# Two fused feed-forward layers behind linear attention on one core: phase 0's out products two units behind, x parts as jobs, phase 1 in another block order, x tiles moved in SBUF

## The chip, the cores and the metric

The kernel runs on one core of one Trainium2 chip. The metric is the device time of one execution in microseconds (us), lower is better: the median of the runs. TensorE is called PE here, VectorE DVE, ScalarE ACT, GpSimd POOL, and SyncE, which here issues DMAs, SP.

## The reference

All inputs are float32. Attention has 8 batches, 8 heads, 576 positions and 64 columns a head, and no softmax; then come two gated feed-forward layers on 4608 tokens of 512 columns, with 1536 hidden columns.

```python
kv = einsum('bhsd,bhse->bhde', k, v)
out = einsum('bhsd,bhde->bhse', q, kv)
x = out / sqrt(mean(out*out, -1) + 1e-6) * g_norm      # then 4608 x 512
x = (sigmoid(x @ moe_w_gate) * (x @ moe_w_val)) @ moe_w_out
y = (silu(x @ moe2_w_gate) * (x @ moe2_w_val)) @ moe2_w_out
```

## The kernel before, in words

**Tiling.** The 4608 tokens are 9 blocks of 512. There are four phases over all blocks (`PH`): phase 0 does hidden columns 0 to 767 of the first layer, phase 1 columns 768 to 1535 of it, phases 2 and 3 the same for the second layer. Each operand is split into a rounded part and a remainder (hi and lo), and each product is three matmuls, lo·hi, hi·lo and hi·hi (`PASSES`). Phase 0 multiplies plainly (`gv_plain`, `part_plain`); phases 1 to 3 do gate and value with seven 2x2 products in place of eight (`gv_win`), and phases 2 and 3 the out product too.

**A unit of phase 0** is one block and one slice of 128 hidden columns, six units a block. Its 24 matmuls (L920) fill two PSUM banks of a ring of four, gate and value; attention's small products take banks of the same ring. ACT makes the sigmoid of the gate bank (L928, tile sg), DVE multiplies it with the value bank (L930), and `split` (L394) then makes the unit's h: hi by ACT (L395), lo by DVE (L373). Only after both ops have read them are the unit's two banks free. The out product of a unit, 12 matmuls (L1104, tile o, from h and wo), is written behind the next unit's gate and value matmuls: `tail` holds the one unit that is still without its out product. There is room for three units' h.

**Order on the engines.** Each engine runs its instructions in order. In blocks 4 to 8 of phase 0 the code sets the order on ACT, DVE and POOL, and a scheduler that of PE and SP; from phase 1 on the code sets PE's order too. The code's own order has two sources. The weights of phases 1 to 3 are rounded and combined by 780 jobs (load, ACT, DVE, POOL, store), which `pump` gives out one at a time: an account (`clock`, `free`, `ready`) keeps estimated times of the engines, and a job is given to an engine once its inputs are expected and it wouldn't wait there. Some jobs may go to DVE or to POOL. The other source are queues of steps with due times; they ask no account. One of them, `xq`, makes x.

**x in phase 0.** Attention writes x of a block to DRAM (`xd`). `seven_steps` loads it in four quarters (tile xl, issued on ACT's own DMA queue, L865), splits each into hi (ACT) and lo (DVE), and for phase 1 subtracts quarters from each other (tile xl, DVE) and stores four results in `x7` (tile name xs, L880). Blocks 3 to 8 do this when they are prepared for phase 0; blocks 0 to 2 are loaded a second time for it, behind blocks 4, 5 and 6.

**x in phases 1 to 3.** Three tiles x0, x1 and x2 hold seven combinations, hi and lo: x0 those named 11, 21 and 22, x1 T1 and T2, x2 T3 and T4. Each of the seven products of a unit reads one combination with 12 matmuls (L1001), x streaming as the moving operand and a weight tile wgv loaded as the stationary one. In the built program x0 begins at byte 163,776 of each partition and x1 at 176,064, both multiples of 64; x2 begins at 221,152, 32 bytes past a multiple of 64. All wgv tiles of these phases begin on multiples of 64.

Of the kernel before, what the change touches and what calls it, by code (L numbers as in the profile page):

```python
# [20 lines left out]
def attention_two_ffn(ctx: ExitStack, tc: tile.TileContext, q, k, v, g_norm, weights, out):  # L21
# [247 lines left out]
    def tok_c(tau):  # L269
        if tau >= XT:  # L270
# [4 lines left out]
            j, c = divmod(tau, TPB)  # L275
            for i in range(P // SQ):
# [11 lines left out]
        j, c = divmod(tau, TPB)  # L288
        cs = slice(c * P, (c + 1) * P)
# [61 lines left out]
    WOUT = (2, 3)  # L351
    phase_of = {(f, m0 + i): (ph, i) for ph, (f, m0, n, _) in enumerate(PH) for i in range(n)}
# [145 lines left out]
    class Job:  # L498
        def __init__(self, does, f, *keys, new=None):
            self.does, self.f, self.keys, self.new = does, f, set(keys), new  # L500
# [24 lines left out]

    def sides():
        if "L" in late:
            return ("B", "C") if now[0] < tick_of(*ASIDE_TO) else ()
# [47 lines left out]
    def pump():  # L576
# [170 lines left out]
    def begin_small():  # L747
# [3 lines left out]
        for z in jobs:  # L751
            if z.group.side is None and z.group not in fresh:
# [53 lines left out]
    def x_load(ph, j, b):  # L806
        k, i = x_at(b)
        h, l = [x_tiles(ph, j)[k][:, i + e] for e in range(2)]
        if PH[ph][0]:
# [39 lines left out]
    def x_steps(ph, j):  # L849
        if PH[ph][3]:  # L850
            return [z for b in (0, 4, 3, 5, 1, 2, 6) for z in (lambda b=b: x_load(ph, j, b), nop)]
        th = seven_steps(j, True, j > 2)
        return th + [nop] + seven_steps(j - 4, False, True) if j in (4, 5, 6) else th

    def seven_steps(j, use_, keep):
        st = {}
        if keep:
            x7[j] = dr.tile([P, 4 * DM], F32, name=f"xs{j}")

        def L(i, n):  # L860
            def run():
                for t in range((j + 1) * TPB):
                    att.need(t)
                st[i, n] = wk.tile([P, 2, HB], F32, tag="xl", bufs=3, name="xl")
                nc.scalar.dma_start(out=st[i, n], in_=xd[0, j][:, 2 * i:2 * i + 2, n * HB:(n + 1) * HB])  # L865
                moved(0.25)
            return run

        def S(i, n):
            def run():  # L870
                hi, lo = [t[:, 2 * i:2 * i + 2, n * HB:(n + 1) * HB] for t in x_tiles(0, j)]
                split(hi, lo, st[i, n])
            return run if use_ else nop

        def D(o, a, b):
            return lambda: sub(st[o], st[a], st[b])

        def store(i, n, o):
            def run():
                nc.sync.dma_start(out=x7[j][:, (o - 3) * DM:(o - 2) * DM], in_=st[i, n].rearrange("p k a -> p (k a)"))  # L880
                moved(0.25)
            return run

        if not keep:
            return [L(0, 0), L(0, 1), L(1, 1)] + [nop] * 6 + [S(0, 0), L(1, 0), nop, S(0, 1), nop, S(1, 1), nop, nop, S(1, 0)]
        return [nop] * LEAD + [L(0, 0), L(0, 1), L(1, 1)] + [nop] * 4 + [S(0, 0), S(0, 1), D((0, 0), (0, 1), (0, 0)), S(1, 1), store(0, 0, 3), D((0, 1), (1, 1), (0, 1)), nop, store(0, 1, 5), L(1, 0),
                D((0, 0), (1, 1), (0, 0)), nop, store(0, 0, 4), nop, S(1, 0), D((1, 0), (1, 0), (0, 0)), nop, store(1, 0, 6)]

# [22 lines left out]
    def gv_plain(ph, j, m, tick):  # L911
# [22 lines left out]
        split(t[:, 0], t[:, 1], sg)  # L934
# [748 lines left out]
```

## Time and profile before

| | us |
|---|---|
| time, median of 3 runs (1797.91 to 1800.07) | 1798.28 |
| time of the profiled execution | 1802.5 |
| its span, first to last instruction | 1800.7 |
| PE busy in it | 1768.0 |
| DVE, ACT and POOL busy | 1221.9, 707.4, 886.4 |

The span is nearly all PE work, so what counts is where PE doesn't run or runs slowly. A matmul's busy time in the rows is its whole passage through the engine, which overlaps with the next one's; the pace is the distance between starts.

### The profile page before, as it was taken

The numbers are of one execution on the slowest core, as the hardware profiler recorded it, in microseconds if no ns is written. First come the engines' busy times: TensorE is split into PE (matmuls) and PEld (weight loads), VectorE is DVE, ScalarE is ACT, GpSimd is POOL, SyncE is SP. The second block draws the span as 40 slices with busy tenths as digits, with TensorE's granted clock in tenths as the row PEclk, the third lists the DMA queues.
The fourth block names the chain that finished last, engine by engine and source line by source line (L and its number), as shares of the span: only waits on it lengthen the run. The fifth ranks groups of instructions, "written<-read, shape, count | busy, mean of one in ns | idle before, by whom it ended". The sixth has DMA issues, their size and how long they took to land.

```text
span 1800.7 us, 33917 instructions
## 1 busy us (share of the span) xinstructions
PE 1768.0 (98%) x12844; PEld 1646.1 (91%) x12844; DVE 1221.9 (68%) x1947; ACT 707.4 (39%) x1535; POOL 886.4 (49%) x960
## 2 busy tenths in 40 slices
PE   7899999999999999999999999999999999999998
PEld 6788888877789999999999999999999999999998
DVE  6764666675674788887775766666665666666665
ACT  4653333233333434443433433333333433333332
POOL 1653455653541467677663444444443444444444
PEclk9999999999999999999999999999999999999999
DMA  9958887669758565656559522222229523223322
GB/s 282 279 162 231 193 236 221 176 198 311 258 189 301 187 216 192 230 180 216 202 205 348 191 65 66 65 66 66 65 90 327 169 89 89 89 89 89 88 89 71
DMA packets 288164, 309.51 MB, mean 172 GB/s; under 512 B 96384, under 2 KB 213504, under 8 KB 287744
## 3 DMA queue, kind: packets, MB, share of 16 engines
q1 hardware_dynamic: 265984, 291.08, 51.0%
q10 hardware_dynamic: 22016, 16.26, 3.1%
q8 instruction: 101, 1.65, 0.4%
q14 instruction: 63, 0.52, 0.1%
HBM read 194.28 MB, written 112.98 MB: 171 GB/s over the span
## 4 chain that ended last, share of the span: by engine, by line
PE 85%; DMA 5%; DVE 4%; POOL 2%; issue 2%; ACT 2%; SPq 1%; ACTq 0%; DVEq 0%; POOLq 0%
PE gv L1001 44%; PE o L1141 14%; PE gv L920 11%; PE o L1119 8%; PE o L1104 6%; PE ops L230 1%; DMA x<-xc 1%; DMA raw<-in_moe_w_out_dram 1%; PE kvps L178 1%; DMA xl<-xd 1%; DMA qm<-in_q_dram 0%; DVE xl L373 0%; DMA aside<-in_moe_w_gate_dram 0%; DMA aside<-in_moe_w_val_dram 0%; POOL aside L651 0%
## 5 line engine op out<-in xcount | busy, mean ns | idle before, releaser
L1001 PE MATMUL gv<-x,wgv 128*128 128x256 f32 x6804 | 827.9, 282 | 3.3 <-ACT u L1010 1.6
L1001 PEld LDWEIGHTS gv<-x,wgv 128*128 128x128 f32 x6804 | 820.4, 191 | 6.3 <-ACT u L1010 1.8
L920 PE MATMUL gv<-x,wgv 128*128 128x512 f32 x1296 | 316.1, 395 | 5.7 <-ACT x L292 2.7
L920 PEld LDWEIGHTS gv<-x,wgv 128*128 128x128 f32 x1296 | 240.9, 189 | 57.7 <-DVE sg L930 4.2
L823 DVE TENSOR_TENSOR x<-x 128x512 fp32r<-128x512 f32 x155 | 147.2, 970 | 45.2 <-ACT x L819 41.3
L1104 PE MATMUL o<-h,wo 128*128 128x512 f32 x648 | 166.5, 401 | 5.9 <-ACT h L395 5.2
L377 DVE TENSOR_TENSOR u<-u,gv 128x512 f32<-128x512 f32 x162 | 110.9, 684 | 85.1 <-ACT h L1044 46.6
L1104 PEld LDWEIGHTS o<-h,wo 128*128 128x128 f32 x648 | 121.3, 191 | 34.7 <-ACT h L395 6.4
L970 ACT ACTIVATE w<-v 128x256 f32<-128x256 f32 x81 | 33.9, 418 | 248.3 <-DVE v L377 244.8
L819 ACT ACTIVATE x<-x 128x512 fp32r<-128x512 f32 x189 | 113.6, 620 | 29.7 <-DMA x<-xc 11.7
L1119 PE MATMUL o<-h,wob 128*128 128x512 f32 x432 | 102.1, 392 | 0.0
L1045 POOL TENSOR_TENSOR spare<-w,spare 128x256 fp32r<-128x256 f32 x54 | 40.8, 755 | 114.2 <-ACT spare L1044 114.2
L1045 POOL TENSOR_TENSOR he<-w,he 128x256 fp32r<-128x256 f32 x54 | 41.0, 759 | 113.7 <-ACT he L1044 113.7
L1045 POOL TENSOR_TENSOR he<-g,he 128x256 fp32r<-128x256 f32 x54 | 50.7, 958 | 92.2 <-ACT he L1044 82.4
L1119 PEld LDWEIGHTS o<-h,wob 128*128 128x128 f32 x432 | 79.8, 188 | 16.6
L1045 POOL TENSOR_TENSOR spare<-g,spare 128x256 fp32r<-128x256 f32 x54 | 50.4, 953 | 90.4 <-ACT spare L1044 90.4
L1010 ACT ACTIVATE u<-gv 128x512 f32<-128x512 f32 x81 | 48.3, 597 | 110.5 <-PE gv L1001 107.5
L1141 PE MATMUL o<-arena,h 128*128 128x256 f32 x636 | 82.9, 279 | 0.0
L377 DVE TENSOR_TENSOR v<-g,gv 128x512 f32<-128x512 f32 x81 | 55.6, 687 | 39.5 <-PE gv L1001 34.8
L970 ACT ACTIVATE v<-g 128x256 f32<-128x256 f32 x81 | 33.9, 418 | 120.9 <-DVE g L377 120.9
L395 ACT ACTIVATE h<-sg 128x512 fp32r<-128x512 f32 x54 | 34.0, 630 | 116.3 <-DVE sg L930 111.5
L1141 PEld LDWEIGHTS o<-arena,h 128*128 128x128 f32 x636 | 78.0, 188 | 0.0
(194 smaller groups left out, 2910.5 us busy)
## 6 DMA issues: line engine op xcount, KB each, us to landing
wgv<-wd SPq DMA_DIRECT2D x72, 448.0 KB, 7.5
x<-xc SPq DMA_DIRECT2D x126, 256.0 KB, 2.8
pl<-pd SPq DMA_DIRECT2D x80, 256.0 KB, 4.2
xc<-pl SPq DMA_DIRECT2D x63, 256.0 KB, 2.3
raw<-in_moe_w_out_dram SPq DMA_DIRECT2D x22, 512.0 KB, 5.0
wd<-stage SPq DMA_DIRECT2D x44, 256.0 KB, 2.2
xl<-xd ACTq DMA_DIRECT2D x40, 256.0 KB, 3.6
wd<-raw SPq DMA_DIRECT2D x39, 256.0 KB, 4.0
```

What stands on the lines that cost most here:

```text
L377: nc.vector.tensor_tensor(out=out, in0=a, in1=b, op=ALU.add)
L395: nc.scalar.activation(hi, src, AF.Copy)
L819: nc.scalar.activation(h, l.bitcast(F32), AF.Copy)
L823: ENG[sooner(0)].tensor_tensor(out=l, in0=l.bitcast(F32), in1=h.bitcast(F32), op=ALU.subtract)
L920: nc.tensor.matmul(ps, w[:, e, a, kk, :], x[b][:, kk, :], start=(n == 0), stop=(n == 3 * KD - 1))
L970: nc.scalar.activation(o, t[:, 0], AF.Silu if f else AF.Sigmoid)
L1001: nc.tensor.matmul(ps[:, e], w[:, l, kk], xs[x_at(r)[0]][:, x_at(r)[1], kk], start=(fresh and e == n == kk == 0), stop=(not more and e == ...
L1010: nc.scalar.activation(u, c1, AF.Copy)
L1045: nc.gpsimd.tensor_tensor(out=hs[z][:, 1], in0=x, in1=hs[z][:, 0].bitcast(F32), op=ALU.subtract)
L1104: nc.tensor.matmul(ps, l, r, start=(fresh and t == 0), stop=(last and t == 2))
L1119: nc.tensor.matmul(ps, l, r, start=(fresh and e == t == 0), stop=(last and e == 1 and t == 2))
L1141: nc.tensor.matmul(ps[:, t], h[:, r, cs], w[:, Ax[a] + 7 * l], start=(start and t == n_ == 0), stop=(stop and t == 1 and n_ == 2), skip_gr ...
```

## The change

Five things are changed. (1) From the fourth visit of phase 0 on (`LAG_FROM`; blocks 0 and 1 are visited twice each, in halves), the out product of a unit stands behind the gate and value matmuls of the second unit after it (`tails`). (2) The split of h is written behind the out product that follows the unit, no longer right behind the multiply. (3) For blocks 3 to 8 the loads, splits, differences and stores of x are jobs of the account, ahead of the weights' jobs (`always`); the lo parts and differences may go to DVE or POOL, and the loads are issued on SP. `x_need` gives out what is left of a block's jobs when the block begins. (4) Phase 1 takes the blocks in the order 3 to 8, 0 to 2 (`blk`); the differences of blocks 0 to 2 are made by 36 jobs at the start of phase 1, not in phase 0. (5) The weights of phase 1's first two slices are allocated ahead of x0 and x1 in their pool. As built, x0 then begins at byte 200,672 and x1 at 212,960, both 32 past a multiple of 64, as x2 does, which stays; the weight tiles still begin on multiples of 64.

```diff
     def open_right():
+        for c in (0, 2):
+            for m in range(PH[1][1], PH[1][1] + NRIGHT):
+                w_tile(0, m, c)
...
+    blk = lambda ph, j: (j + 3) % NBLK if ph == 1 else j
...
     def sides():
         if "L" in late:
-            return ("B", "C") if now[0] < tick_of(*ASIDE_TO) else ()
+            return ("B",) if n_always() else ("B", "C") if now[0] < tick_of(*ASIDE_TO) else ()
...
-        while len(jobs) > floor:
+        while jobs:
             held_keys, best = set(), None
-            for n, z in enumerate(jobs[:WINDOW]):
+            n_x = n_always()
+            for n, z in enumerate(jobs[:n_x + WINDOW] if len(jobs) - n_x > floor else jobs[:n_x]):
...
+                    if z.when is not None:
+                        r = max(r, max(landed.get(t, 9e9) for t in range((z.when + 1) * TPB)))
...
+    def x_jobs(j, use_):
...
+                nc.sync.dma_start(out=st[p], in_=xd[0, j][:, 2 * i:2 * i + 2, n * HB:(n + 1) * HB])
+            J({"D": 0.25}, run, p)
...
+            J({"A": 0.62}, lambda: nc.scalar.activation(part[0](), st[p], AF.Copy), p)
+            J({"V": 0.72, "G": 1.4}, lambda e: ENG[e].tensor_tensor(out=part[1](), in0=st[p], in1=part[0]().bitcast(F32), op=ALU.subtract), p)
+        def D(o, a, b, q):
+            J({"V": 0.72, "G": 1.4}, lambda e: ENG[e].tensor_tensor(out=st[o], in0=st[a], in1=st[b], op=ALU.subtract), o, a, b)
+            J({"D": 0.25}, lambda: nc.sync.dma_start(out=x7[j][:, (q - 3) * DM:(q - 2) * DM], in_=st[o].rearrange("p k a -> p (k a)")), o)
...
+    def x_need(j):
+        while any(z.of == ("x", j) for z in jobs):
+            emit(jobs[0], next(iter(jobs[0].does)), clock[0])
...
-        split(t[:, 0], t[:, 1], sg)
+        return nop, lambda: split(t[:, 0], t[:, 1], sg)
...
+                tail = None if ph == 0 and at_ >= LAG_FROM and len(tails) < 2 or not tails else tails.pop(0)
...
-                tail = (ph, j, m)
+                tails.append((ph, j, m))
...
+            for z in range(3):
+                x_put(z)
```

On PE, in block 7 of phase 0, at the end of the unit with weight slice 3 (wgv0_3; wo0_2 is the out weight of slice 2). Before:

```order
L920 MATMUL gv_4803<-x0_4339,wgv0_3_1025 128x512
L1104 MATMUL o_4696<-h_110,wo0_2_933 128x512 x3
L1104 MATMUL o_4701<-h_110,wo0_2_933 128x512 x3
L1104 MATMUL o_4706<-h_110,wo0_2_933 128x512 x3
L1104 MATMUL o_4713<-h_110,wo0_2_933 128x512 x3
L920 MATMUL gv_4847<-x0_4339,wgv0_4_1273 128x512
```

After, at the same place:

```order
L972 MATMUL gv_4787<-x0_4186,wgv0_3_1023 128x512
L1156 MATMUL o_4744<-h_110,wo0_1_663 128x512 x3
L1156 MATMUL o_4748<-h_110,wo0_1_663 128x512 x3
L1156 MATMUL o_4754<-h_110,wo0_1_663 128x512 x3
L1156 MATMUL o_4759<-h_110,wo0_1_663 128x512 x3
L972 MATMUL gv_4833<-x0_4186,wgv0_4_1271 128x512
```

Behind slice 3's gate and value stood the out product of slice 2; now that of slice 1 stands there.

On DVE, the stretch ahead of the multiply of block 7's slice 2 (aside, u and s are tiles of weight jobs, x1 the lo tile of block 8's x). Before:

```order
L449 TENSOR_SCALAR aside_4148<-aside_4148 128x512
L454 SCALAR_TENSOR_TENSOR aside_4148<-aside_4148 128x512
L459 TENSOR_SCALAR aside_4149<-aside_4148 128x512
L463 SCALAR_TENSOR_TENSOR aside_4149<-aside_4148,aside_4149 128x512
L373 TENSOR_TENSOR x1_4738<-xl_4651,x0_4737 128x2x256
L373 TENSOR_TENSOR x1_4738<-xl_4658,x0_4737 128x2x256
L449 TENSOR_SCALAR aside_4148<-aside_4148 128x512
L454 SCALAR_TENSOR_TENSOR aside_4148<-aside_4148 128x512
L930 TENSOR_TENSOR sg_1719<-sg_1719,gv_4744 128x512
L373 TENSOR_TENSOR h_110<-sg_1719,h_110 128x512
L373 TENSOR_TENSOR xl_4651<-xl_4658,xl_4651 128x512
```

After, the stretch around the same slice's multiply (gv_4719):

```order
L465 TENSOR_SCALAR s_4740<-u_4647 128x512
L982 TENSOR_TENSOR sg_1719<-sg_1719,gv_4719 128x512
L469 SCALAR_TENSOR_TENSOR s_4740<-raw_4614,s_4740 128x512
L379 TENSOR_TENSOR h_110<-sg_1719,h_110 128x512
L473 TENSOR_TENSOR u_4647<-u_4647,s_4740 128x512
L667 TENSOR_TENSOR s_4776<-u_4647 128x256
L667 TENSOR_TENSOR s_4776<-s_4776,u_4608 128x256
L913 TENSOR_TENSOR x1_4595<-xl_4736,x0_4594 128x2x256
```

The lo of h no longer follows the multiply directly, and one part of x stands in this stretch where there were two parts and a difference.

## Rows read from the trace of the kernel before

**Rows 1.** The page: span; costliest groups: count | busy us, mean ns | idle before.
```profile
span 1800.7 us, 33917 instructions
...
L1001 PE MATMUL gv<-x,wgv 128*128 128x256 f32 x6804 | 827.9, 282 | 3.3 <-ACT u L1010 1.6
...
L1141 PE MATMUL o<-arena,h 128*128 128x256 f32 x636 | 82.9, 279 | 0.0
```

**Rows 2.** Busy time by stretch: length, then PE, PEld, DVE, ACT, POOL, granted clock, DMA.
```profile
100.00:350.00 250.00, 250.00 (x1516) 209.17 (x1515) 154.81 (x233) 91.81 (x165) 128.43 (x184) 1.00 0.77 207
350.00:505.00 155.00, 146.14 (x618) 115.83 (x617) 108.41 (x142) 54.53 (x100) 80.94 (x77) 0.98 0.72 235
...
565.00:985.00 420.00, 419.29 (x2932) 392.78 (x2931) 312.80 (x474) 165.03 (x332) 259.08 (x208) 1.00 0.65 224
```

**Rows 3.** Groups on PE, 350 to 505 us: busy, mean ns, idle before, releasers.
```profile
L920 PE MATMUL gv<-x,wgv 128*128 128x512 f32 x408 | 96.7, 391 | 2.9 <-DVE sg L930 2.6 <-ACT sg L928 0.4
L1104 PE MATMUL o<-h,wo 128*128 128x512 f32 x202 | 54.0, 414 | 5.9 <-ACT h L395 5.2 <-ACT ye L1349 0.4 <-DVE h L373 0.2
L230 PE MATMUL ops<-kvz,qT 128*128 128x128 f32 x8 | 1.1, 274 | 0.0
```

**Rows 4.** Timeline, 426 to 500 us: start, length, engine, line, operation, count, idle before.
```profile
429.19 4.79 PE L1104 MATMUL o<-h,wo 128*128 128x512 f32 x12 [2.10 <-ACT h L395]
...
485.63 5.60 PE L920 MATMUL gv<-x,wgv 128*128 128x512 f32 x24
...
487.51 0.68 ACT L444 ACTIVATE aside<-aside 128x512 f32<-128x512 f32 x1 [2.05 <-DMA aside<-in_moe_w_out_dram]
...
488.09 0.58 ACT L928 ACTIVATE sg<-gv 128x512 f32<-128x512 f32 x1
...
491.39 0.68 DVE L930 TENSOR_TENSOR sg<-sg,gv 128x512 f32<-128x512 f32 x1
...
492.78 0.51 PE L1104 MATMUL o<-h,wo 128*128 128x512 f32 x1 [1.55 <-ACT h L395]
```

**Rows 5.** Two stretches: length, PE busy, granted clock, DMA share, GB/s.
```profile
429.00:433.00 4.00, 3.81 (x9) 0.57 0.87 255
...
494.00:498.00 4.00, 4.00 (x13) 0.57 0.59 215
```

**Rows 6.** Waits of PE, 505 us to the end: us in total, times, longest.
```profile
PE gv L1001 <- ACT u L1010: 1.6, 1, 1.6
PE gv L1001 <- POOL x L823: 1.0, 1, 1.0
PE gv L1001 <- DVE v L377: 0.7, 1, 0.7
```

**Rows 7.** Groups on DVE, 350 to 505 us: differences and lo parts of x.
```profile
L373 DVE TENSOR_TENSOR xl<-xl 128x512 f32<-128x512 f32 x15 | 15.6, 1040 | 0.1
...
L373 DVE TENSOR_TENSOR x<-xl,x 128x512 fp32r<-128x512 f32 x11 | 9.4, 854 | 4.7 <-ACT x L395 4.6
```

**Rows 8.** Timeline of PE in one unit of phase 2, by product.
```profile
1201.58 1.47 PE L1001 MATMUL gv<-x,wgv 128*128 128x256 f32 x11
...
1203.01 2.92 PE L1001 MATMUL gv<-x,wgv 128*128 128x256 f32 x23
...
1205.89 1.46 PE L1001 MATMUL gv<-x,wgv 128*128 128x256 f32 x11
...
1207.19 2.92 PE L1001 MATMUL gv<-x,wgv 128*128 128x256 f32 x23
...
1210.06 0.86 PE L1141 MATMUL o<-wob,he 128*128 128x256 f32 x6
```

**Rows 9.** The page's DMA issues: count, size of one, median us to landing.
```profile
xl<-xd ACTq DMA_DIRECT2D x40, 256.0 KB, 3.6
```

**Rows 10.** Waits of SP's queue, 350 to 500 us: us in total, times, longest.
```profile
SPq L1360 <- ACT ye L1349: 11.3, 3, 9.0
```

**Rows 11.** A group on POOL, 350 to 505 us.
```profile
L651 POOL TENSOR_TENSOR raw<-u,raw 128x512 fp32r<-128x512 f32 (+1 forms) x9 | 12.4, 1380 | 5.0 <-ACT raw L655 5.0
```

More of the change, by code (lines that the diff above doesn't have):

```diff
@@ L275, in tok_c @@
             j, c = divmod(tau, TPB)
+            landed[tau] = clock[0] + 6.0
             for i in range(P // SQ):
@@ L288, in tok_c @@
         j, c = divmod(tau, TPB)
+        landed[tau] = clock[0] + 6.0
         cs = slice(c * P, (c + 1) * P)
@@ L499, in __init__ @@
         def __init__(self, does, f, *keys, new=None):
-            self.does, self.f, self.keys, self.new = does, f, set(keys), new
+            self.does, self.f, self.keys, self.new, self.when = does, f, set(keys), new, None
     jobs, ready, rings, aside = [], {}, {}, {}
@@ L524, in buf, with n_always @@
             return x.rearrange("p (a b) -> p a b", b=2) if t == "raw" else x.bitcast(F32)
+    always = Group()
+    always.side = "X"
+    landed = {}
+    def n_always():
+        return sum(z.group is always for z in jobs)
     def sides():
         if "L" in late:
-            return ("B", "C") if now[0] < tick_of(*ASIDE_TO) else ()
+            return ("B",) if n_always() else ("B", "C") if now[0] < tick_of(*ASIDE_TO) else ()
         return ("R",) if "R" in late and clock[0] < ASIDE[0] else ()
@@ L751, in begin_small @@
         for z in jobs:
-            if z.group.side is None and z.group not in fresh:
+            if z.group.side is None and z.group is not always and z.group not in fresh:
                 fresh.append(z.group)
@@ L851, in x_steps, with load, sp, J @@
             return [z for b in (0, 4, 3, 5, 1, 2, 6) for z in (lambda b=b: x_load(ph, j, b), nop)]
[L852 to L860, printed above, removed]
+        st, th = {}, []
+        def load(i, n):
+            for t in range((j + 1) * TPB):
+                att.need(t)
+            st[i, n] = wk.tile([P, 2, HB], F32, tag="xl", bufs=3, name="xl")
+            nc.scalar.dma_start(out=st[i, n], in_=xd[0, j][:, 2 * i:2 * i + 2, n * HB:(n + 1) * HB])
+            moved(0.25)
+        def sp(i, n):
+            hi, lo = [t[:, 2 * i:2 * i + 2, n * HB:(n + 1) * HB] for t in x_tiles(0, j)]
+            split(hi, lo, st[i, n])
+        L, S = [{o: lambda o=o, z=z: z(*o) for o in ((0, 0), (0, 1), (1, 1), (1, 0))} for z in (load, sp)]
+        return [L[0, 0], L[0, 1], L[1, 1]] + [nop] * 6 + [S[0, 0], L[1, 0], nop, S[0, 1], nop, S[1, 1], nop, nop, S[1, 0]]
+    def x_jobs(j, use_):
+        st, out = {}, []
+        x7[j] = dr.tile([P, 4 * DM], F32, name=f"xs{j}")
+        slot = {(0, 0): 0, (0, 1): 1, (1, 1): 2, (1, 0): 1}
+        def J(does, f_, *ps):
+            out.append(Job(does, f_, *[("xl", slot[p]) for p in ps]))
+            out[-1].of, out[-1].group = ("x", j), always
+        def L(p):
+            i, n = p
             def run():
@@ L863, in run @@
                     att.need(t)
[L864 to L887, printed above, removed]
+                st[p] = wk.tile([P, 2, HB], F32, tag="xl", bufs=3, name="xl")
@@ new lines, in run, with S @@
+                nc.sync.dma_start(out=st[p], in_=xd[0, j][:, 2 * i:2 * i + 2, n * HB:(n + 1) * HB])
+            J({"D": 0.25}, run, p)
+            out[-1].when = j
+        def S(p):
+            i, n = p
+            if not use_:
+                return
+            part = [lambda z=z: x_tiles(0, j)[z][:, 2 * i:2 * i + 2, n * HB:(n + 1) * HB] for z in range(2)]
+            J({"A": 0.62}, lambda: nc.scalar.activation(part[0](), st[p], AF.Copy), p)
+            J({"V": 0.72, "G": 1.4}, lambda e: ENG[e].tensor_tensor(out=part[1](), in0=st[p], in1=part[0]().bitcast(F32), op=ALU.subtract), p)
@@ L889, in comp_steps, with x_put @@
+        D(p00, p11, p00, 4)
+        L(p10)
+        S(p10)
+        D(p10, p10, p00, 6)
+        return out
+    def x_put(j):
+        new = x_jobs(j, True) if j > 2 else x_jobs(j, False)
+        k = sum(z.group is always for z in jobs)
+        jobs[k:k] = new
+    def x_need(j):
+        while any(z.of == ("x", j) for z in jobs):
+            emit(jobs[0], next(iter(jobs[0].does)), clock[0])
     def comp_steps(j, st):
@@ L1342, in evac @@
             if i == 1:
-                th = comp_steps(j, {divmod(z, 2): part.pop((ph, j, z)) for z in range(4)})
+                th = comp_steps(blk(ph, j), {divmod(z, 2): part.pop((ph, j, z)) for z in range(4)})
                 for k, z in enumerate(th):
@@ L1579, in attention_two_ffn @@
                     queued = True
-                    xq.put(tick_of(*nxt, 0) - 3, ([nop] * 8 if first else []) + x_steps(*nxt), nxt)
+                    if nxt[0] == 0 and nxt[1] > 2:
+                        x_put(nxt[1])
+                    else:
+                        xq.put(tick_of(*nxt, 0) - 3, ([nop] * 8 if first else []) + x_steps(*nxt), nxt)
                 m = m0 + i
```

23 lines of the change are left out of this document (18 added, 5 removed).

## The prediction

> **What bounds the kernel now.** The page comes first: PE is busy for 1768 of the 1800.7 us of the span [rows 1], so the kernel is as fast as PE is fed and clocked, and work taken off another engine is worth only what PE waits for it. Next come the stretches. From 100 to 350 us PE is never idle; from 350 to 505, the second half of phase 0, it is idle for 155 - 146.1 = 8.9 us and its clock falls [rows 2]. Behind 505 us the waits of PE add up to 3.3 us in three places [rows 6]. The first 100 us, the start of attention, also hold waits, but the change doesn't reach them: the lag begins with the fourth visit, and the x of blocks 0 to 2 is made as before.
>
> So there are two things to read closely: the stretch from 350 to 505 us, and the pace at which PE runs where it waits for nothing.
>
> The stretch first. In a quiet place 24 gate and value matmuls take 5.60 us, of which the last one's passage is 0.39, so the pace is (5.60 - 0.39) / 23 = 0.2265 us [rows 3, 4]. The 408 + 202 matmuls of the stretch would need 610 x 0.2265 = 138.2 us and attention's eight 1.1 [rows 3]; 155 - 139.3 = 15.7 us are lost. Of these 8.8 are waits that the rows name, 5.9 ahead of out products and 2.9 ahead of gate and value [rows 3]. Right behind two of the out product's waits the granted clock is 0.57 over 4 us, so PE ran at the lower of its levels, 1.2 instead of 2.4 GHz, for part of it, which costs 2 x 4 x 0.43 = 3.4 us [rows 4, 5]. The other 3.5 are restarts, since a wait also bares the passage of the matmul ahead of it, and gaps too short to be listed.
>
> How such a wait arises is seen at 488 us [rows 4]. ACT stands at a weight job (aside) until 487.51, because its DMA came later than the account believed. The sigmoid behind it starts at 488.09, though its bank was complete before the next unit began at 485.63; the multiply on DVE, behind the job's other steps and two lo parts of x, follows at 491.39, h behind that, and PE, which has run through the whole next unit meanwhile, stands 1.55 us. This wait and the one at 429 us, 2.10, are waits for h.
>
> **The change, part by part.** *Out products two units behind, h given out later.* Nothing is added on PE; 12 matmuls change places with 24. An h now has the gate and value and one out product more, 36 x 0.2265 = 8.2 us, before it is wanted. The longest wait for an h in the stretch is 2.1 us [rows 4], so I take all of them as gone, the later split included: it is queued behind the out product of the same unit, 12 x 0.2265 = 2.7 us, and 8.2 covers that too. That gives back 5.5 us of idle time (the 5.9 without the 0.4 for ACT's copy of an output), the 3.4 of the clock, and 5.5 / 8.8 of the 3.5 for restarts, 2.2: together 11.1. If the cover is gone, up to all of this stays.
>
> *x as jobs.* The 2.9 us ahead of gate and value are waits for a PSUM bank, which DVE's late multiply frees. There the lag helps nothing: a bank is wanted again as early as before. What helps is a DVE that is less behind. In the stretch it spends 15.6 us on 15 differences of x, 1040 ns each, and 9.4 on 11 lo parts, ahead of which it stood 4.6 us for ACT [rows 7]; the queue of steps put them there without asking whether DVE had time. As jobs they wait their turn, some go to POOL, and the second makings for blocks 0 to 2 (12 differences, 12.5 us of DVE at that price) leave phase 0. But weight jobs fill some of the room, and a 128x512 subtraction takes POOL 1380 ns [rows 11]. Between 0 and all of it (2.9 and 3.5 x 2.9 / 8.8 = 1.2 for restarts, 4.1) I take half, 2.0: a DMA that is late for ACT, as in rows 4, stays as it is. Phase 0 then gives 11.1 + 2.0 = 13.1, at most 15.7.
>
> The loads leave ACT's queue for SP's and stand there behind its waits, the longest of which is 9.0 us [rows 10]; what hides that is that a block's x is begun a block ahead. In the order of the built program the last part of x stands two to three units, 16 us or more, ahead of its block's first matmul, and only for block 3 right at it; I cost it at nothing, and more under the rivals.
>
> *Block order.* The 36 jobs for blocks 0 to 2 come into phase 1, where DVE is busy 312.8 of 420 us and POOL 259.1 [rows 2] and where one wait of PE for POOL, 1.0 us at the end of that stretch, is all there is [rows 6]. They are wanted only by the seventh visit. Bounds: 0 and, if that wait doubles, 1.0; I take 0. Which blocks phase 2 begins with doesn't change, and their input is done two visits earlier or more.
>
> *x tiles 32 bytes on.* This touches all of phases 1 to 3. The rows of one unit are cut so that each begins inside or at the head of a product, and distances between their starts give the pace [rows 8]. From 1203.01, the second matmul on x1, to 1205.89, the second on x2, are 24 matmuls in 2.88 us: 120.0 ns each on x1. From there to 1207.19, the first on x0 again, are 11 in 1.30: 118.2 on x2. On x0 it is 12 in 1.43 and 24 in 2.87, 119.4 together. Same operation, same engine, same 256 columns; what differs is that x2 begins 32 bytes off the multiple of 64 at which the weights and the other two x tiles begin. After the change x0 and x1 lie as x2 does. Of the 6804 matmuls [rows 1] three sevenths read x0, 2916, and two sevenths x1, 1944: 2916 x 1.2 + 1944 x 1.8 ns = 3.5 + 3.5 = 7.0 us. Bounds: 0, if the pace belongs to the product and not to the place of its tile, and 3 ns on 4860 matmuls, 14.6 us, if they come to the passage of the out products, 279 against 282 ns [rows 1], where the two operands also lie 32 bytes apart. I take 7.0, the row nearest to it in kind.
>
> The Trainium skill speaks against this term: its page "SBUF — State Buffer", section "SBUF: two separate sides", lets engines contend for SBUF only at the port pair that VectorE and GpSimd share, and says that PE never waits on anyone; no place of a tile would then change PE's pace. "TensorE: Matmul & The Clock Gate", section "Wait — 56ns, not 53.3ns?", gives 256 columns 256 / 2.4 + 2.5 = 109.2 ns, an estimate from that page, below every pace in rows 8. By these pages the term is 0 instead of 7.0.
>
> Sum: 13.1 + 7.0 = 20.1 us. The profiled execution's own time is 1802.5 us, 1.8 more than its span, and would become 1782.4. The median of the runs is 4.2 below it, and I take the same 20.1 off it: 1798.3 - 20.1 = **1778.2 us**.
>
> **Rivals.** *The place of x does nothing.* T3 and T4 might run faster for another reason, say what stands ahead of them. For it: one sort of tile at one place is all the evidence. Against it: x1's 23 matmuls are even and slow, and x2's two products aren't neighbours. Time: 1798.3 - 13.1 = 1785.2. This is what the page on SBUF would have.
>
> *The wait moves to the banks.* PE no longer stands for h, runs on, and stands at the gate and value of the second unit after, because the multiply that frees its bank is as late as it was. In rows 4 the next unit but one would have begun at 485.63 + 36 x 0.2265 = 493.8 and its bank came free at 491.39 + 0.68 = 492.1: 1.7 us of room. Where DVE is later than that, the wait is back. If half of the 11.1 comes back and the half of the bank's waits isn't saved either, phase 0 gives 5.5: 1798.3 - 5.5 - 7.0 = 1785.8; with the first rival too, 1792.8.
>
> *Slower: x arrives late.* A load on SP stands behind a wait of 9.0 us [rows 10], takes 3.6 to land [rows 9], then come ACT's hi, about as long as its 0.68 on the same size [rows 4], and POOL's lo, 1.4 [rows 11]: 14.7 us. The six blocks 3 to 8 can't begin without their last part. Against it is the lead of 16 us. If the engines run so far behind the order that each beginning loses 5 us, the change ends at 1778.2 + 30 = 1808; it decides from 20.1 / 6 = 3.4 us a beginning.
>
> **How the numbers follow.** The forecast, both gains within some 5 us: 0.62. The place does nothing: 0.12. The wait moves: 0.13. Both of these, or gains cancelled by new waits, so that the time is within 0.2%: 0.06. x late: 0.07. A measurement of this kernel can tell about 0.2%, 3.6 us, from no change. Faster by more is 0.62 + 0.12 + 0.13 and a little of the next, 0.88; within it 0.05, slower 0.07. The range goes down to 1770, the whole 15.7 with an alignment gain somewhat past 12, and up to 1790, which takes in the first two rivals and leaves out both together and the slower one.
>
> **What would show it.** In the profile after: no wait of out products for h from 350 to 505 us and a clock of 1.00 there; waits of gate and value for the multiply of some 1.5 us (3 or more: the second rival). One product on x1 with passages of about 280 instead of 283 ns, and phases 1 to 3 shorter by 7 us; if they are as long as before, the first rival. First matmuls of a block that wait for x, by ACT, DVE or POOL, would be the third. I am wrong if phases 1 to 3 show new waits of PE, of which the rows of before give no sign.

## The result, and the profile after

The changed kernel takes **1775.57 us** (median of 4 runs, 1774.0 to 1776.97), the kernel before beside it 1799.03 (4 runs); the ratio is 0.9869, interval 0.9852 to 0.9887. Forecast were 1778.2 us. Times and ratios leave out two executions that took several times as long as the others of their kernel, 9473.9 us (e3_w_off, the traced one) and 4589.0 us (e9_w0_off). The profiled execution of after took 1775.2 us, its span is 1773.3. Two groups of the page, against [rows 1]: count | busy us, mean ns | idle before.

```profile
span 1773.3 us, 33959 instructions
...
L1053 PE MATMUL gv<-x,wgv 128*128 128x256 f32 x6804 | 812.4, 280 | 4.4 <-ACT u L1062 2.6
...
L1156 PE MATMUL o<-h,wo 128*128 128x512 f32 x648 | 163.3, 397 | 3.9 <-ACT ye L1401 2.8
```

L1053 is what L1001 was: the same 6804 matmuls are busy for 812.4 us in place of 827.9, at 280 ns of passage in place of 282. So most of the gain, 15.5 us of busy time, lies in a row that has no new instruction and no lost one.

**Where the time went.** The first matmul of each phase, before and after, by its start in the trace: phase 1 at 565.7 and 555.2 us, phase 2 at 979.8 and 962.3, phase 3 at 1380.6 and 1358.0, the last matmul of all at 1795.7 and 1768.6. So 10.5 us are gained up to phase 1, then 7.0, 5.1 and 4.5 in phases 1, 2 and 3. At the start of phase 1 both kernels have begun the same matmuls; inside phase 0, from the lag on, the changed kernel is one out product behind, 12 matmuls or 2.7 us.

Not all of the 10.5 us belong to the change. The lag begins with the tenth unit of phase 0. The seventh unit, the first of the third visit, and the first unit of phase 1, in before and then in after:

```profile
120.05 2.23 PE L920 MATMUL gv<-x,wgv 128*128 128x512 f32 x9
...
565.75 4.48 PE L1001 MATMUL gv<-x,wgv 128*128 128x256 f32 x36
```
```profile
118.13 3.14 PE L972 MATMUL gv<-x,wgv 128*128 128x512 f32 x13
...
555.16 3.08 PE L1053 MATMUL gv<-x,wgv 128*128 128x256 f32 x25
```

Between the two stand the same 2220 matmuls in every trace used here. They take 445.7 us before and 437.0 after: 8.7 us are gained there, and the other 1.9 ahead of it. This stretch serves below to compare phase 0.

**Phase 0.** PE's waits from 250 to 505 us in after, in full, and two stretches (length, PE, PEld, DVE, ACT, POOL, granted clock, DMA share, GB/s):

```profile
PE o L1156 <- ACT ye L1401: 2.8, 1, 2.8
PE gv L972 <- DVE sg L982: 0.8, 1, 0.8
```
```profile
472.00:476.00 4.00, 3.98 (x11) 2.81 (x10) 2.08 (x3) 3.48 (x8) 4.00 (x3) 0.57 1.02 358
350.00:505.00 155.00, 151.39 (x662) 124.22 (x661) 113.11 (x135) 61.30 (x113) 110.61 (x96) 0.99 0.78 254
```

From 350 to 505 us PE is idle for 3.6 us, where it was 8.9 [rows 2], and begins 662 matmuls in place of 618. Not one wait for h is left. What is left is of the same make, one step further on. The timeline of after (start, length, engine, line, operation, count, idle before):

```profile
470.07 0.67 ACT L450 ACTIVATE u<-raw 128x512 f32<-128x512 f32 x1 [3.27 <-DMA raw<-in_moe_w_gate_dram]
...
470.94 0.59 ACT L1401 ACTIVATE ye<-o 128x512 f32<-128x512 f32 x1
...
471.58 4.82 PE L1156 MATMUL o<-h,wo 128*128 128x512 f32 x12 [2.84 <-ACT ye L1401]
```

ACT stands 3.27 us at a weight job whose DMA is late, as at 487 us in [rows 4]. Behind that job now waits not an h that PE wants, but the copy that empties a PSUM bank of the out products; PE wants the bank and stands 2.84 us. The granted clock behind it is 0.57 over 4 us: PE's lower level, 1.2 GHz, for a part of it, as in [rows 5].

**Phases 1 to 3.** A unit of gate and value there is 84 matmuls, 81 units in all. PE in one unit of phase 2, first with x0 and x1 at their old places (e1_x_back, told of below, in which the rest is as in after), then in after:

```profile
1165.35 10.18 PE L1050 MATMUL gv<-x,wgv 128*128 128x256 f32 x84
1175.36 2.99 PE L1190 MATMUL o<-arena,he 128*128 128x256 f32 x24
```
```profile
1156.30 9.97 PE L1053 MATMUL gv<-x,wgv 128*128 128x256 f32 x84
1166.10 2.96 PE L1193 MATMUL o<-arena,he 128*128 128x256 f32 x24
```

From the unit's first matmul to the one behind its last: 1175.36 - 1165.35 = 10.01 us, and 1166.10 - 1156.30 = 9.80. PE waits for nothing in either. 81 x 0.21 = 17.0 us.

**What was given back.** At the start of phase 3 PE waits for ACT's copy of a gate bank, as before, 1.6 us [rows 6], but longer, and now the clock falls behind it. PE's rows of before, then those of after:

```profile
1388.16 3.13 PE L1001 MATMUL gv<-x,wgv 128*128 128x256 f32 x24 [1.64 <-ACT u L1010]
```
```profile
1366.40 4.62 PE L1053 MATMUL gv<-x,wgv 128*128 128x256 f32 x24 [2.61 <-ACT u L1062]
```
```profile
1366.00:1370.00 4.00, 3.60 (x18) 3.60 (x19) 3.33 (x5) 1.78 (x5) 4.00 (x5) 0.58 1.04 410
```

1.0 us more of waiting and 4.62 - 3.13 = 1.5 us more for the same 24 matmuls at a granted clock of 0.58: 2.5 us. Against it, the wait of 0.7 us for DVE's v, which stood close behind in the trace of before [rows 6], is gone, so 1.8 us are given back. That is most of why phase 3 gains less. At phase 2's start the wait for POOL's x grew by 0.7.

### The profile page after: what moved, and what is told of

It reads as the page before. It is cut to its first block, busy times and chain, and to the rows that moved or that the text cites. A ratio compares the mean times of both kernels' runs of the same rounds, so it can differ in the third digit from the quotient of the medians.

```text
span 1773.3 us, 33959 instructions
## 1 busy us (share of the span) xinstructions
PE 1744.9 (98%) x12844; PEld 1628.0 (92%) x12844; DVE 1211.9 (68%) x1904; ACT 707.9 (40%) x1535; POOL 937.9 (53%) x1003
## 4 chain that ended last, share of the span: by engine, by line
PE 85%; DMA 6%; DVE 3%; POOL 2%; issue 2%; ACT 1%; SPq 1%; DVEq 0%; POOLq 0%; ACTq 0%
PE gv L1053 44%; PE o L1193 14%; PE gv L972 10%; PE o L1171 8%; PE o L1156 5%; PE ops L233 1%; DMA raw<-in_moe_w_out_dram 1%; DMA raw<-in_moe_w_gate_dram 1%; DMA x<-xc 1%; DMA raw<-in_moe_w_val_dram 1%; DMA wd<-raw 1%; DMA qm<-in_q_dram 0%; PE kvps L181 0%; DVE u L460 0%; POOL y L247 0%
## 5 line engine op out<-in xcount | busy, mean ns | idle before, releaser
L1053 PE MATMUL gv<-x,wgv 128*128 128x256 f32 x6804 | 812.4, 280 | 4.4 <-ACT u L1062 2.6
L1053 PEld LDWEIGHTS gv<-x,wgv 128*128 128x128 f32 x6804 | 804.9, 188 | 7.4 <-ACT u L1062 2.8
L972 PEld LDWEIGHTS gv<-x,wgv 128*128 128x128 f32 x1296 | 241.2, 189 | 54.2 <-issue 1.8
L842 DVE TENSOR_TENSOR x<-x 128x512 fp32r<-128x512 f32 x157 | 150.9, 981 | 46.8 <-ACT x L838 38.7
L383 DVE TENSOR_TENSOR pl<-pl,o 128x256 f32<-128x256 f32 (+1 forms) x106 | 49.3, 502 | 39.4 <-PE o L1193 23.1
## 6 DMA issues: line engine op xcount, KB each, us to landing
x<-xc SPq DMA_DIRECT2D x126, 256.0 KB, 2.8
pl<-pd SPq DMA_DIRECT2D x80, 256.0 KB, 4.1
xc<-pl SPq DMA_DIRECT2D x63, 256.0 KB, 2.6
wd<-raw SPq DMA_DIRECT2D x42, 256.0 KB, 3.2
wd<-stage SPq DMA_DIRECT2D x39, 256.0 KB, 2.2
pd<-ye SPq DMA_DIRECT2D x36, 256.0 KB, 3.9
```

The source lines that it names most:

```text
L383: nc.vector.tensor_tensor(out=out, in0=a, in1=b, op=ALU.add)
L842: ENG[sooner(0)].tensor_tensor(out=l, in0=l.bitcast(F32), in1=h.bitcast(F32), op=ALU.subtract)
L972: nc.tensor.matmul(ps, w[:, e, a, kk, :], x[b][:, kk, :], start=(n == 0), stop=(n == 3 * KD - 1))
L1053: nc.tensor.matmul(ps[:, e], w[:, l, kk], xs[x_at(r)[0]][:, x_at(r)[1], kk], start=(fresh and e == n == kk == 0), stop=(not more and e == ...
```

## The experiments on the place of x

**e1_x_back**: the changed kernel with x0 and x1 back on multiples of 64; all other parts of the change stay.

```diff
-        for c in (0, 2):
-            for m in range(PH[1][1], PH[1][1] + NRIGHT):
-                w_tile(0, m, c)
```

> The changed kernel with x0 and x1 put back on multiples of 64 bytes (the weights of phase 1's first slices are again allocated behind them); all else as changed. Changed kernel: phases 1 to 3 took 1213 us against 1230 before, gate and value matmuls start every 116.7 to 116.9 ns against 119.5 (x0), 120.0 (x1), 118.1 (x2). Theory 'place' (the pace hangs on where the x tiles begin): the old paces come back, x2's too, and the kernel takes 16 to 17 us longer than the changed one, about 1792. Rival 'schedule' (the pace comes from what the other parts moved on DVE, POOL and the DMA queues): the paces stay near 117 and the time near 1775.

1793.77 us, 0.9976 (0.9967 to 0.9986). So the place is worth 1793.8 - 1775.6 = 18.2 us in the changed kernel (by the two ratios, each to the kernel before beside it, 19.2), and the four other parts together 0.24% of 1797.0, 4.3 us. Distances between starts, averaged over all matmuls of phases 1 to 3 that follow one another without a wait and at the full clock, are 119.5, 120.0 and 118.1 ns on x0, x1 and x2, as before; in after they are 116.85, 116.68 and 116.69. That gives 2916 x 2.67 + 1944 x 3.32 + 1944 x 1.45 ns = 7.8 + 6.5 + 2.8 = 17.1 us, which agrees with the medians.

**e2_pad, e4_x0_only, e3_w_off** change the kernel before. The first two put a strip of 32 bytes behind x1, or behind x0, so that both, or x0 alone, begin 32 bytes lower. The third leaves x alone and puts the weights of slices 2 to 5 of each phase 32 bytes lower.

```diff
+                    late["R"].tile([P, LINE], U32, name="gap_r")
```
```diff
-    H_AT, ARENA_AT, W7_AT = 3 * LINE, LINE, LINE
-    RIGHT, LEFT = {(1, 0): (0, LINE)}, {2: 3 * LINE}
+    H_AT, ARENA_AT, W7_AT = 3 * LINE, 2 * LINE, LINE
+    RIGHT, LEFT = {(1, 0): (0, LINE)}, {2: 2 * LINE}
```

> The kernel before with one unused strip of 32 bytes behind x1, which moves x0 and x1 down by 32 bytes (163,744 and 176,032, both 32 past a multiple of 64); weights, x2 and the order of all instructions stay. 'Place': paces of 116.7 to 117 on x0, x1 and also on x2, phases 1 to 3 shorter by 16 to 17 us, about 1782; the waits between 350 and 505 us stay. 'Schedule': no change, 1799. My forecast's own sizing (x0 and x1 come to x2's old pace and no further): 7 us, 1792.

1788.27 us, 0.9947 (0.9932 to 0.9961). The paces are 118.0, 118.3 and 117.0 ns. The unit, against 10.01 and 9.80 us above, takes 1174.02 - 1164.12 = 9.90:

```profile
1164.12 10.06 PE L1002 MATMUL gv<-x,wgv 128*128 128x256 f32 x84
1174.02 2.99 PE L1142 MATMUL o<-arena,he 128*128 128x256 f32 x24
```

So 32 bytes lower isn't 32 bytes higher: it is no question of being off the multiples of 64 alone. And x2, which did not move, is faster, 117.0 in place of 118.1.

> The kernel before with the unused strip of 32 bytes behind x0, which moves x0 alone down by 32 bytes; x1 stays on a multiple of 64. 'Place': x0 at about 117, x1 at 120.0; 2916 x 2.7 ns = 8 us faster, 1791. What it tells besides: x2's first product of a unit stands right behind x1's two. If x2 was held back by x1's pace ahead of it, it stays at 118 here; if by x0's, it comes to 117.

1792.26 us, 0.9974 (0.9964 to 0.9984); 118.1, 119.9 and 117.8 ns. x1 stays slow where it lies, x0 gains by its own place, and x2 gains a little again. A tile's pace thus hangs on its place, and x2's also on how fast its neighbours in the unit run.

> The kernel before with the gate and value weights of slices 2 to 5 of phases 1 to 3 moved down by 32 bytes, so that they begin 32 past a multiple of 64; x0 and x1 stay on multiples of 64, x2 stays 32 past one; slices 0 and 1 stay. 'Relative place' (slow where the stationary and the moving operand have the same remainder of 64): in two thirds of the units x0 and x1 get fast (about 117) and x2 slow (about 120); net about 2/3 x (2916 x 2.7 + 1944 x 3.3 - 1944 x 1.9) ns = 7 us faster, 1792. 'Own place' (a moving tile on a multiple of 64 is slow whatever the weights do): no change, 1799.

1789.8 us, 0.9956 (0.9942 to 0.997). It is read by its times alone. x did not move, and 7 us are gained: the place of the weights counts as well.

**e9_w0_off and e10_w_off** move weights in the changed kernel: those of phase 0 by 32 bytes, where x and weights began at the same remainder of 128; and those of slices 2 to 5 of phases 1 to 3, as e3 did (there x and weights then begin at one remainder of 64 again).

```diff
-    FIRST = {(0, 0): 4 * LINE}
+    FIRST = {(0, 0): 3 * LINE, (5, 1): (0, LINE)}
```

This is e9's edit; e10's is the one shown for e3.

> The changed kernel with all weights of phase 0, those of gate and value and those of the out product, 32 bytes lower, so that they begin on multiples of 64 while x and h of phase 0 begin 32 past one; before and after, operands in phase 0 have the same remainder and matmuls of 512 columns start every 227 ns. 'Relative place' (the pace is lost where both operands have the same remainder): 1944 matmuls of 512 columns gain some 3 ns each, phase 0 and the kernel get about 6 us faster, 1770. 'Own place' (only a moving tile on a multiple of 64 is slow): phase 0's moving tiles were never on one, and nothing changes, 1776.

1781.23 us, 0.9908 (0.9891 to 0.9924). The change of pace is clear, and of the other sign than in phases 1 to 3. PE's units of phase 0 in after, then in this kernel:

```profile
430.50 5.60 PE L972 MATMUL gv<-x,wgv 128*128 128x512 f32 x24
...
438.66 5.60 PE L972 MATMUL gv<-x,wgv 128*128 128x512 f32 x24
```
```profile
437.45 5.76 PE L972 MATMUL gv<-x,wgv 128*128 128x512 f32 x24
...
445.85 5.76 PE L972 MATMUL gv<-x,wgv 128*128 128x512 f32 x24
```

36 matmuls take 8.40 us in place of 8.16, 233.3 ns in place of 226.7. Over 54 units that is 13.0 us, of which 5.7 show in the time (7.0 by the ratios): a slower PE waits less. From 90 to 560 us its trace has one wait of PE, 0.4 us, where after has 4.5 in four.

> The changed kernel with the gate and value weights of slices 2 to 5 of phases 1 to 3 moved down by 32 bytes, to the same remainder of 64 as the x tiles; slices 0 and 1 stay and are the control in the same trace. 'Relative place': slices 2 to 5 go to 119 to 120 ns on all three x tiles, slices 0 and 1 stay near 117; 4536 x 3 ns = 13.6 us slower, about 1789. 'Own place': nothing changes, 1776.

1781.87 us, 0.9909 (0.9888 to 0.9929). Slices 2 to 5 run at 117.8, 117.7 and 117.6 ns, slices 0 and 1, whose weights stayed, at 116.8, 116.7 and 116.8 as in after. Slower, but far from 120: the same remainder of 64 is not what makes 120.

**e11_x32 and e12_x0** move x0 and x1 in the changed kernel by 64 and by 96 bytes down; the weights of slices 0 and 1, which lie below x, go down by 128 with them. The strips are (2, 2) and (1, 3) times 32 bytes.

```diff
+                    late["R"].tile([P, 2 * LINE], U32, name="gap_w")
                     for k in range(2):
                         aside[f"x{k}"] = late["R"].tile(...)
+                    late["R"].tile([P, 2 * LINE], U32, name="gap_x")
```

> The changed kernel with x0 and x1 at bytes 32 past a multiple of 128 instead of 96 past one; the weights stay 64 past one. If all that counts is that x is off the multiples of 64 and the weights on them, paces stay at 116.7 ns and the time at 1775.6 us. If 32 and 96 differ, as the 118.0 to 118.3 ns of e2_pad and e4_x0_only say, x0 and x1 are at 118.0 to 118.3, and the time is 1775.6 + 2916 x 1.3 + 1944 x 1.6 ns = 1782.5. If the neighbours' pace was behind those, it lies between.

1787.67 us, 0.9949 (0.9929 to 0.9969), slower than either reading had it. By weights the paces on x1 are 120.0 ns in slices 0 and 1 and 118.2 to 118.4 in slices 2 to 5. The weights of both groups begin at the same remainder of 128, so this modulus is too small.

> The changed kernel with x0 and x1 on multiples of 128, the weights 64 past one, x2 still 96 past one. If it counts that both operands begin on multiples of 64, the pace is back at 119.5 to 120.0 ns on x0 and x1 and some 118 on x2, and the time at 1792. If it counts that x begins at the same byte of 128 as the weights, which these places avoid, the pace is near 116.7 and the time near 1776.

1777.08 us, 0.9876 (0.986 to 0.9893), not apart from after. That both begin on multiples of 64 does no harm here: on x1 the pace is 117.8 ns in slices 0 and 1 and 114.8 on average in slices 2 to 5. Two units of phase 2, of slices 2 and 3 and of 4 and 5:

```profile
1163.88 10.03 PE L1055 MATMUL gv<-x,wgv 128*128 128x256 f32 x84
1173.75 2.98 PE L1195 MATMUL o<-arena,he 128*128 128x256 f32 x24
1176.57 9.80 PE L1055 MATMUL gv<-x,wgv 128*128 128x256 f32 x84
1186.21 2.98 PE L1195 MATMUL o<-arena,spare 128*128 128x256 f32 x24
```

9.87 and 9.64 us; in phases 2 and 3 the two change places nearly from block to block. So the 114.8 ns is a mean that no unit runs at. PE's timeline cut at matmuls on x1 or just behind, as in [rows 8], 24 matmuls from line to line, in the first of these units and then in the second:

```profile
1165.41 2.99 PE L1055 MATMUL gv<-x,wgv 128*128 128x256 f32 x24
...
1168.24 0.51 PE L1055 MATMUL gv<-x,wgv 128*128 128x256 f32 x3
```
```profile
1177.94 0.62 PE L1055 MATMUL gv<-x,wgv 128*128 128x256 f32 x4
...
1180.66 0.52 PE L1055 MATMUL gv<-x,wgv 128*128 128x256 f32 x3
```

2.83 / 24 = 117.8 ns and 2.72 / 24 = 113.3 ns. Of the 54 units of slices 2 to 5, 36 run at 113.3 ns on x1, all 18 of phase 1 among them, and 18 at 117.8. In phases 2 and 3 it is the same unit, with x, weights and PSUM banks at the same bytes in the built program, that goes at one pace in one block and at the other in the next. Other kernels have single strays of this kind: one of after's 81 units, at 1023.83 us, runs at 117.7 ns, and one of e10's in slices 2 to 5, at 565.8, at 113.3.

The mean paces, 116.2, 115.8 and 117.2 ns, would give 2.5 us on after, which is within the interval. The traced execution, 1782.8 us, is 5.7 above the median; its seventh unit begins only at 125.0 us.

**What the eight say together.** (e3, read by its times alone, and e9, which is of phase 0, aren't in the table.) Sorted by where x begins past where the weights begin, modulo 256 (from the built programs' addresses), the pace on x1 is

| distance | kernels (slices) | ns |
|---|---|---|
| 0 | before, e1, e4 | 119.9 to 120.0 |
| 32 | after, e10 (0, 1) | 116.6 to 116.7 |
| 64 | e10 (2 to 5), e12 (0, 1) | 117.6 to 117.8 |
| 96 | e11 (0, 1) | 120.0 |
| 192 | e12 (2 to 5) | 113.3 in 36 units, 117.8 in 18 |
| 224 | e2, e11 (2 to 5) | 118.2 to 118.4 |

Distance 64 comes from two different pairs of remainders (224 and 160, 128 and 64), and the two agree to 0.2 ns. The table was made after the runs: that the distance decides is a reading which fits, not one that was foretold and then met. It is not the whole either: the units of e12 alternate between two paces at one distance, x2 at distance 32 has 118.1 ns in before and 116.7 in after, and at 512 columns, phase 0, distance 0 is the fast one (226.7 ns in after) and 32 the slow one (233.3 in e9), the other way about than here.

## The experiments on the schedule

**e5_no_lag**: the changed kernel without the lag, and with the split right behind the multiply.

```diff
-        return nop, lambda: split(t[:, 0], t[:, 1], sg)
+        split(t[:, 0], t[:, 1], sg)
...
-    LAG_FROM = 3
+    LAG_FROM = 1000
```

> The changed kernel without the lag: each out product again behind the next unit's gate and value, h again split right behind the multiply; x as jobs, the block order and the x tiles as changed. Changed kernel: from the 25th unit to the start of phase 1 262.1 us; kernels with the old phase 0 took 266.2 to 269.6. Theory 'lag' (what phase 0 gained came from giving h more time): out products wait for h again in two or three places, that stretch takes 5 us longer or more, the kernel about 1781. Rival 'jobs' (it came from x being placed by the account, which keeps DVE and ACT on time): the stretch stays within 2 us and the kernel within 3 us of the changed one.

1784.29 us, 0.9925 (0.9908 to 0.9942): the lag is worth 8.7 us in this surrounding (10 by the ratios). PE's waits of its trace from 250 to 560 us, then from 560 us on:

```profile
PE o L1156 <- ACT ye L1401: 2.8, 1, 2.8
PE o L1156 <- DVE h L379: 2.3, 2, 1.1
PE o L1156 <- ACT h L401: 1.2, 1, 1.2
```
```profile
PE gv L1053 <- POOL x L842: 3.9, 1, 3.9
PE gv L1053 <- ACT u L1062: 1.9, 1, 1.9
PE gv L1053 <- DVE v L383: 1.2, 2, 1.0
PE gv L1053 <- DVE u L383: 0.6, 1, 0.6
```

The waits for h are back, 3.5 us, and phase 1 begins 3.5 us later than in after (558.7). But from the seventh unit to phase 1 it takes 438.4 us, after 437.0: only 1.4 of the 3.5 us stand where the lag acts. The rest stands ahead of the seventh unit, where only the place of the split differs and where traces of one order differ by more. So the time of the kernel is nearer to the expectation's theory, while phase 0 goes the rival's way: the stretch from the 25th unit, 260.9 us and after 262.1, with the lag's 2.7 us of matmuls in the latter alone, stays within 2 us. Most of what phase 0 gained is there without the lag. The other 5 us are in phases 1 and 2, 2.8 and 3.3 us longer, in waits that the lag has no direct part in: the account, which runs on from phase 0, gives the jobs out in another order.

**e7_x_steps**: the changed kernel with x of blocks 3 to 8 made by the old queue of steps, its loads on ACT's queue again. Lag, block order and the second makings of blocks 0 to 2 in phase 1 stay.

```diff
-                    if nxt[0] == 0 and nxt[1] > 2:
-                        x_put(nxt[1])
-                    else:
-                        xq.put(tick_of(*nxt, 0) - 3, ([nop] * 8 if first else []) + x_steps(*nxt), nxt)
+                    xq.put(tick_of(*nxt, 0) - 3, ([nop] * 8 if first else []) + x_steps(*nxt), nxt)
...
```

The old `seven_steps`, which comes back with it, isn't shown.

> The changed kernel with the x of blocks 3 to 8 made by the old queue of steps (loads on ACT's queue, lo parts and differences on DVE); lag, block order, the 36 jobs in phase 1 and the x tiles as changed. 'Lag': the stretch from the 25th unit to phase 1 takes 262 to 265 us, since h has the room; what comes back are at most the waits of gate and value for the multiply, 2.6 us in the trace of before. 'Jobs': it takes 267 us or more.

1775.69 us, 0.9869 (0.9852 to 0.9885): the same. From the seventh unit to phase 1 it takes 436.7 us. That x parts of blocks 3 to 8 are jobs gives nothing that can be measured.

**e6_lag_only**: the kernel before with the lag and the later split alone.

```diff
-        split(t[:, 0], t[:, 1], sg)
+        return nop, lambda: split(t[:, 0], t[:, 1], sg)
...
+                tail = None if ph == 0 and at_ >= 3 and len(tails) < 2 or not tails else tails.pop(0)
...
-                tail = (ph, j, m)
+                tails.append((ph, j, m))
...
```

> The kernel before with the lag of the out products and the later split of h alone; x by the old queue of steps, old block order, old places. If the lag carries phase 0's gain, phase 1 begins some 7 us earlier than in the traces with the old phase 0 (562.7 us on average), at about 556, and the time is 1790 to 1792 us with paces of 119.5, 120.0 and 118.1 ns. If the gain needs the account's x jobs too, phase 1 begins at 560 or later and the time is 1795 to 1798. If the account's new job order in phases 1 and 2 is what cost e1_x_back the rest of its gain, this kernel ends below e1_x_back's ratio of 0.9976.

1802.92 us, 1.0029 (1.0018 to 1.004): alone, the lag makes the kernel **slower**, by 5 us, outside both expectations; phase 1 begins at 570.2 us, 448.3 behind the start of the seventh unit, where before has 445.7. PE's waits from 250 to 505 us, and how the longest comes about:

```profile
PE o L1104 <- ACT ye L1349: 3.6, 3, 2.0
PE o L1104 <- ACT h L395: 3.5, 1, 3.5
PE gv L920 <- DVE sg L930: 3.0, 3, 2.1
PE gv L920 <- ACT sg L928: 1.9, 2, 1.1
```
```profile
446.75 0.68 DVE L930 TENSOR_TENSOR sg<-sg,gv 128x512 f32<-128x512 f32 x1
...
454.25 0.66 ACT L444 ACTIVATE aside<-aside 128x512 f32<-128x512 f32 x1 [6.70 <-DMA aside<-in_moe_w_gate_dram]
...
458.92 0.61 ACT L395 ACTIVATE h<-sg 128x512 fp32r<-128x512 f32 x1
...
459.59 0.49 PE L1104 MATMUL o<-h,wo 128*128 128x512 f32 x1 [3.49 <-ACT h L395]
```

The multiply is done at 447.4 us, and ACT makes the h at 458.92, 11.5 us later: it stands 6.70 us at one weight job and 3.46 at the next (458.36). The lag's cover of 8.2 us is smaller than that. The other waits are for banks, which the lag does not help.

With e1, e5 and e7 this makes a picture of parts that do not add. The lag alone costs 5 us; with block order and x jobs it becomes e1's gain of 4.3; the x jobs of blocks 3 to 8 give nothing there (e7), and without the lag phase 0 loses only 1.4 us behind the seventh unit (e5). What is left to turn the one into the other is the block order, which takes the second loads, differences and stores of blocks 0 to 2 out of phase 0, and the account's knowledge of when attention's x has landed. This is by elimination; no run has the block order alone.

**e8_late**: the changed kernel with an account that expects DMAs 4.0 us late in place of 2.0.

```diff
-    LATE, AHEAD_D, BUBBLE, STEP = 2.0, 2.0, {"A": 0.3, "V": 0.3, "G": 0.5}, 0.2
+    LATE, AHEAD_D, BUBBLE, STEP = 4.0, 2.0, {"A": 0.3, "V": 0.3, "G": 0.5}, 0.2
```

> The changed kernel with one constant of the account: a DMA is expected 4.0 us behind its issue in place of 2.0. If weight jobs given out ahead of their DMAs cause what is left of waits in phase 0 (the 2.8 us of an out bank behind ACT's copy, and the half clock behind it), that wait goes and the time falls by 3 to 5 us, to 1771 to 1773. If the jobs then pile up and are late for the phases behind, phases 1 to 3 show new waits and the time is 1776 or more.

1789.73 us, 0.9951 (0.9936 to 0.9965). The wait goes, as the first half of the expectation says; the time follows the second half. From 250 to 560 us PE has no listed wait at all and from 350 to 505 it is busy throughout, at a clock of 1.00:

```profile
350.00:505.00 155.00, 155.00 (x694) 128.62 (x693) 105.76 (x126) 59.70 (x107) 104.42 (x92) 1.00 0.74 242
```

From the 25th unit of phase 0 to phase 1 it takes 256.0 us, after 262.1, and from the seventh 431.1 in place of 437.0. (Phase 1 still begins 1.5 us later than in after, since the seventh unit begins only at 125.5 us in this trace.) So late DMAs of the account's jobs do cause what is left in phase 0, about 6 us. But the jobs that are held back there stand in the way later. PE's waits behind 560 us:

```profile
PE gv L1053 <- ACT u L1062: 6.4, 3, 3.6
PE gv L1053 <- POOL x L842: 3.0, 1, 3.0
PE gv L1053 <- DVE v L383: 2.6, 5, 1.0
PE gv L1053 <- DVE u L383: 2.3, 2, 1.5
```

14.3 us; phase 1 lasts 419.8 us in place of 407.2. Phase 0's idle time and phase 1's are one account.

## Why the prediction was right, and where it was wrong

The time came out 2.6 us below the forecast, inside the range, with two terms wrong in opposite directions: phase 0 was taken nearly twice too large, the place of x not half large enough. That the sum came so near is luck. Together 7.5 + 17.1 - 1.8 - 0.7, the last two at the starts of phases 3 and 2, are 22.1 of the 23.5 us between the medians; the 1.4 left over are within the interval.

**Phase 0, 13.1 forecast, about 7.5 measured.** Phase 1 begins at 565.7, 560.6 and 561.7 us in the traces that have phase 0 as before (before, e2, e4) and at 555.2, 556.6, 556.0, 553.3 and 560.5 in those that have it as after (after, e1, e10, e11, e12): 562.7 - 556.3 = 6.4 us on average, with a spread of 5 to 7 us in each group. In the second group nearly all of it stands ahead of the seventh unit, which begins between 118.1 and 125.0 us. From there to phase 1 the first three take 445.7, 442.9 and 442.8 us, the other five 437.0, 437.2, 436.6, 435.1 and 435.5: 443.8 - 436.3 = 7.5 us on average, and the groups do not overlap. The trace of before, on whose 8.8 us of waits the sum rests, is the longest of its three. The step that failed is "I take all of them as gone", with the 11.1 us that it gave the lag. It set the cover of 8.2 us against the longest wait of an order that the change does away with. In e6 the new order has an ACT that stands 10 us at two weight jobs, and the lag alone loses 5 us; taken out of the changed kernel (e5), it costs 1.4 us from the seventh unit to phase 1. In after the h are in time, but the out banks are not: 2.8 us, and 4 x 0.43 = 1.7 for the clock behind.

**x as jobs, 2.0 forecast, nothing measured** for blocks 3 to 8 (e7). The remark beside it, that 12 differences for blocks 0 to 2 leave phase 0, was counted into the 2.0 and is likely to be the larger part of all that phase 0 gained, by the elimination above; no run has it alone.

**Block order, 0 forecast, bounds 0 to 1.0.** The wait for POOL's x at phase 2 went from 1.0 to 1.7 us, within them. Not foreseen was the start of phase 3, 1.8 us. The prediction named new waits in phases 1 to 3 as a sign of being wrong; these are the old two, grown. The one at phase 3 is no matter of PE's pace: e1, with the old pace, waits 3.0 us there too. Nor does the block order settle it: e6, with the old one, waits 2.1, and e9 and e10, with the new one, 1.6 as before. What sets its length stays open.

**Place of x, 7.0 forecast, 17 measured.** Direction, sort of row and method were right, the size was not. The forecast gave x0 and x1 the pace of x2, 118.2 ns [rows 8], as the pace of that place. But this row was measured with x2 beside slow neighbours: at its unmoved place x2 runs at 118.1, 117.8, 117.0 and 116.7 ns as x0 and then x1 too become faster (before, e4, e2, after). So the places together are worth 2.7 and 3.3 ns where 1.2 and 1.8 were taken, and the 1944 matmuls on x2, which stood in no term, gave 2.8 us. The upper bound of 14.6 left them out as well, and was too low for it.

**The rivals.** *The place does nothing* is refuted: e1 is 18 us slower than after. How the place acts is not shown. The page "SBUF — State Buffer" of the Trainium skill, section "SBUF: two separate sides", by which PE never waits on anyone, doesn't cover this: the pace moved between 113.3 and 120.0 ns with no wait of PE, and which paces came up went by the places of operands. *The wait moves to the banks* came true in part, at another bank: not gate and value's (0.8 us), but the out product's, by ACT's copy. *x arrives late* did not: in phase 0 no first matmul of blocks 3 to 8 waits for x in after; only e7, with the old steps, shows 0.8 us.

## What to carry to other kernels

Before trusting that PE is at its pace, take distances between starts for each operand tile by itself: 3 ns on 6804 matmuls were worth more here than all waits of PE in the rows. Then look at single units, since a mean can hide two paces, as 114.8 ns hid 113.3 and 117.8. Don't price a reordering by the waits of one trace of the old order: the lag that was to gain 11 us lost 5 alone and gained 9 in company, hardly any of it in the stretch that it was meant for. And where an account or a queue hands out background work, follow a job that is removed or delayed to where it reappears before counting the gain.

## What the runs showed of the hardware that was not expected

With 256 columns, the same matmul with the same shape and types, and PE waiting for nothing, went in 113.3 to 120.0 ns, by the places in SBUF of moving and stationary operand relative to each other and, less, by the pace of its neighbours; with 512 columns in 226.7 or 233.3. 32 bytes one way and 32 bytes the other give different paces (116.7 and 118.3), and moving the weights does what moving x does. The order by distance modulo 256 fits the mean paces on x1 at 256 columns, and the two distances tried at 512 go the other way about; the place alone doesn't fix a pace, since the same unit of e12 runs at 113.3 or at 117.8 ns on x1 with its operands at the same bytes. What decides, and why they alternate, stays open. If every unit could run at 9.64 us, 81 x 0.16 = 13 us more would be had; that is an estimate from e12's rows, and it was not run.
